# Another 20-product scheme for the first matmul of a convolution + GELU network, on one Trainium2 core

## The chip, the cores and the metric

The kernel runs on one core of one Trainium2 chip. The metric is the device time of one launch in microseconds (us). Engines are named as the profile names them: PE is TensorE (matmuls), PEld its weight loads, DVE is VectorE, ACT is ScalarE, POOL is GpSimd, SP is the queue that issues most DMA transfers. All data is float32. A matmul writes into a bank of the accumulation memory; there are eight banks, and here they go in four pairs. DVE and ACT read and write banks and ordinary memory; POOL and DMA only ordinary memory.

## The reference

```python
def _attn_ref(x, weight):            # x (8, 4096, 192), weight (8, 7)
    ...                              # softmax of each head's 7 taps
    out = np.einsum('hk,bskhg->bshg', w, x_unf)   # causal convolution of 7 taps
    return out.reshape(B, S, D)

def _moe_ref(x, w_in, w_out):        # x (32768, 192), w_in (192, 2048), w_out (2048, 192)
    h = x @ w_in
    g = h * (1.0 / (1.0 + np.exp(-1.702 * h)))
    return g @ w_out
```

A short convolution along the sequence, then a product with a 192 x 2048 matrix, a GELU, and a product with a 2048 x 192 matrix.

## The kernel before, in words

**Steps.** The 32768 tokens are done in 32 steps ("bigs") of 1024 tokens. A step has two parts: the first product with its GELUs (line 597), and the second product (line 1021). Step 0 and the start of step 1 are written out separately (`first_step`) and also prepare the weights. From step 2 on all steps have the same instructions.

**The first product by a fast scheme.** It is a product of block matrices of the convolved input (`conv_t`, blocks 0 to 5) by blocks of `w_in`, done twice in a step: half v = 0 and half v = 1 of the hidden columns. In place of 24 block products a half does 20, after a scheme of the Strassen kind: `TERMS[t]` says which combination of weights (`w_in_s`) is multiplied with which combination of input blocks. The combinations of input blocks are formed once a step on POOL (`SUMS_C`, called "vsum" in the lists; blocks 6 and up), those of weights once a launch on DVE (`SUMS_W`). One of the six input blocks (`OPEN`) is needed one half earlier than the others by the next step; one (`UNUSED`) enters sums only. Each block is also copied to the other 64 partitions by DMA (`cross`, on SP), because one product is two matmuls, each on 64 rows of the array:

```python
for h in range(2):
    src = pair[halves[h], ::-1, :] if h else pair[halves[h], :, :]
    nc.tensor.matmul(slot[h], w_in_s[halves[h], a, v * P : (v + 1) * P], src, start=first, stop=True, ...)
```

The two matmuls of a product write the two banks of a pair, h = 0 and h = 1. In float32 each matmul takes two passes, so one product is four PE and four PEld records.

**The list FIRST.** What is done with the products stands in `FIRST`, in the order in which it is issued, with names a0, a1, ... for pairs of banks and k0, k1, ... for places in memory (`room`, given by `ROOM_OF`). `("prod", t, a)` adds product t into a pair. `("copy", dst, src, sign)` copies a pair of banks on ACT, two instructions at line 632; copied to a place k it is kept for a later sum, copied to another pair a it becomes the seed on which further products accumulate. `("sum", dst, a, op, b)` adds or subtracts on DVE, two instructions at line 638. `("gelu", ...)` is on ACT: two instructions (line 614) from a pair of banks, one instruction of 1024 columns (line 619) from a place k. When a pair of banks has been used for the last time it goes to a list of free pairs, first in first out. Each engine works through its own queue in the order of issue and waits on semaphores. The first number of an item says how far ahead it is issued: an item with 1 or 2 is issued inside the half before, so that half v + 1 begins while half v ends; at the turn of a step the items with 1 wait until after the second part.

**Other work between the items.** `FILL[v]` says before which item of FIRST what else is issued: "tap" (one ACT multiplication of the convolution for a later step, line 488), "add" (a POOL addition of such taps, line 506), "vsum" (a POOL sum of blocks), "turn" (a DVE transpose of input, line 443; it also brings the rest of the taps and the end of the convolution, with the `cross` of the OPEN block, if they are still to be issued), "g" (a sum of GELU results for the second product, 128 x 1024 on DVE; one of the five is an accumulating DMA issued by POOL), "cross" (the DMA copies).

**The second part** goes through `PLAN`, a list of the same manner: 78 "go" (three main matmuls and a side matmul each), DVE sums and joins, ACT copies and taps. It takes three pairs of banks, in the order of the list of free pairs: the first is used by the first main and side matmuls at once. At its end up to all but the last of the remaining taps are issued.

Of the kernel before, what the change touches and what calls it, by code (L numbers as in the profile page):

```python
# [15 lines left out]
def kernel(  # L16
# [80 lines left out]
    g = consts.tile([P, NG, 2, 2, NG, T], F32)  # L97
# [29 lines left out]
    def kept(i):  # L127
# [11 lines left out]
    NV = 11  # L139
    NB = NBLK + NV  # L140
    UNUSED = 4
    OPEN = 2
    OPEN_SUM = None
# [5 lines left out]
        (6, 0, "-", 4), (7, 6, "-", 5), (8, 1, "+", 7), (9, 3, "+", 8), (10, 0, "-", 7), (11, 9, "-", 6),  # L149
        (12, 2, "-", 10), (13, 2, "-", 4), (14, 13, "+", 11), (15, 0, "+", 14), (16, 14, "-", 1),  # L150
# [15 lines left out]
    def side(big, other, b):  # L166
# [13 lines left out]
        (13, 9), (6, 14), (9, 0), (14, 5), (11, 6), (7, 2), (1, 3), (15, 3), (0, 0), (4, 16), (16, 8), (10, 2),  # L180
        (17, 15), (18, 7), (2, 11), (8, 12), (3, 1), (12, 1), (5, 10), (19, 13),
# [319 lines left out]
    tree, adds = [], []  # L501
# [138 lines left out]
    def plain(u, m, n, v, slot, ks=range(NC), first=0):  # L640

        for k in ks:
# [15 lines left out]
    ]  # L658
    ROOM_OF = ((0, 4, 1, 1, 4, 4, 4), (3, 0, 2, 2, 0, 2, 1))
# [3 lines left out]
            0: (("tap",),), 1: (("add", 4),), 2: (("add", 4), ("tap",)), 6: (("add", 4),), 11: (("turn", 0),),  # L663
            25: (("turn", 1),), 30: (("turn", 2),),
        },
        {
            0: (("g", 0), ("vsum",)), 1: (("vsum",), ("vsum",)), 2: (("vsum",),), 6: (("vsum",),), 7: (("vsum",),),
            14: (("g", 1), ("vsum",)), 15: (("g", 2),), 19: (("g", 3), ("vsum",), ("vsum",)), 21: (("g", 4),),
            22: (("vsum",),), 26: (("vsum",),), 38: (("cross",),),
# [4 lines left out]
            0: (("add", 12),), 1: (("work", 0.8),), 10: (("work", 0.8), ("tap",)), 15: (("work", 0.8),),  # L674
            19: (("tap",),), 21: (("work", 0.8),), 25: (("tap",),), 27: (("work", 0.8),), 30: (("tap",), ("tap",)),
            31: (("work", 0.8),), 38: (("tap",),), 40: (("tap",),), 42: (("work", 0.8),),
        },
        {
            5: (("g", 0),), 6: (("g", 1),), 13: (("turn", 0),), 19: (("g", 2), ("g", 3)), 21: (("g", 4),),
            26: (("turn", 1),), 27: (("turn", 2),),  # L680
# [259 lines left out]
    def store(big, n, o=None, queues=(nc.sync,) * 3):  # L940
# [16 lines left out]
        ("sum", 14, 14, "-", 18), ("side", 13, 16, "k0"), ("main", 1, 5, "p2", 1), ("vsum",), ("go", 2), ("tap",),  # L957
# [13 lines left out]
        ("sum", 6, 9, "-", 5), ("acc", 18, 14), ("tap",), ("go", 1), ("main", 20, 0, "p1", 0), ("tap",), ("go", 1),  # L971
# [8 lines left out]
        ("main", 8, 8, "p1", 0, 0, 2), ("tap",), ("tap",), ("tap",), ("tap",), ("tree",), ("go", 1),  # L980
# [10 lines left out]
        ("turn", 1, 1, 0, "k8"), ("store", 1, 0),  # L991
    ]
# [360 lines left out]
```

## Time and profile before

| what | value |
|---|---|
| median of 3 runs | 2288.6 us (2288.19 to 2289.3) |
| the profiled execution | 2288.38 us; its span in the trace 2286.6 us; granted PE clock 0.996 |
| PE busy | 2265.5 us, 99% |
| PEld busy | 1352.9 us, 59% |
| DVE busy | 1897.3 us, 83% |
| ACT busy | 1778.2 us, 78% |
| POOL busy | 1062.4 us, 46% |

In rows of groups and of the timeline, a line gives the kernel's line, engine, operation, written and read tiles, shape and count; then busy time and mean duration, or start and duration; and the idle time before with what ended it ("<-ACT room L632": the wait ended when line 632 on ACT had written room). "x2" is two merged instructions.

### The profile page before, as it was taken

The page shows a single profiled execution, that of the slowest core. Times are in us where ns is not written, and L with a number is a line of the kernel's source. Part 1 is how long each engine was busy: PE and PEld are TensorE (multiplying, and loading weights), DVE is VectorE, ACT ScalarE, POOL GpSimd, SP SyncE. Part 2 cuts the span into 40 slices and gives each one's busy share as a digit, 9 for nine tenths or more (in the row PEclk, how much of TensorE's full clock was granted, in tenths as well). Part 3 has the DMA queues.
Part 4 walks back from the last instruction along what each step waited for, and adds up shares of the span by engine and source line. Part 5 has one row for each costly group of instructions (what it writes and reads, how often), then busy time and mean ns, then how long its engine had stood idle before and what let it go on. Part 6 is the DMA issues. An engine that isn't in the chain of part 4 may idle for free.

```text
span 2286.6 us, 62092 instructions
## 1 busy us (share of the span) xinstructions
PE 2265.5 (99%) x24966; PEld 1352.9 (59%) x24966; DVE 1897.3 (83%) x2842; ACT 1778.2 (78%) x3481; POOL 1062.4 (46%) x1101
## 2 busy tenths in 40 slices
PE   9899999999999999999999999999999999999999
PEld 5356656666556566566665566665666655666655
DVE  8798888877888878888878888788888788887788
ACT  8568878788877788787788777887777887778855
POOL 1445544555435555445554355554455544555410
PEclk9899999999999999999999999999999999999999
DMA  9966577666586665776665866666766658664543
GB/s 200 156 146 137 113 141 148 131 126 122 115 161 135 128 127 114 139 147 133 128 123 112 161 138 126 126 116 135 151 133 127 123 112 159 139 128 99 104 94 71
DMA packets 281072, 298.84 MB, mean 131 GB/s; under 512 B 120144, under 2 KB 212304, under 8 KB 280784
## 3 DMA queue, kind: packets, MB, share of 16 engines
q0 software_dynamic: 58080, 151.48, 36.8%
q1 hardware_dynamic: 221056, 143.00, 28.0%
q8 instruction: 197, 3.23, 0.6%
q14 instruction: 91, 0.75, 0.1%
q10 hardware_dynamic: 1648, 0.39, 0.1%
HBM read 53.15 MB, written 25.17 MB: 34 GB/s over the span
## 4 chain that ended last, share of the span: by engine, by line
PE 95%; DVE 3%; ACT 1%; DMA 1%; issue 0%; SPq 0%; DVEq 0%; ACTq 0%
PE slot L597 48%; PE slot L1021 45%; PE slot L839 1%; DMA xin<-in_x_dram 0%; DVE g L363 0%; PE slot L844 0%; DVE xt L443 0%; ACT g L614 0%; DMA w_in_s<-in_moe_w_out_dram 0%; DVE w_in_s L363 0%; DVE conv_t L474 0%; DMA conv_t<-conv_t 0%; ACT w_form L488 0%; DVE slot L638 0%; ACT room L632 0%
## 5 line engine op out<-in xcount | busy, mean ns | idle before, releaser
L597 PE MATMUL slot<-conv_t,w_in_s 64*128 64x512 f32 x5152 | 1165.1, 599 | 3.9 <-ACT room L632 2.3
L597 PEld LDWEIGHTS slot<-conv_t,w_in_s 64*128 64x128 f32 x5152 | 700.2, 186 | 455.9 <-issue 227.3
L1021 PE MATMUL slot<-g,w_form 128*32 128x256 f32 x9672 | 896.0, 380 | 3.4 <-DVE room L361 3.4
L1021 PEld LDWEIGHTS slot<-g,w_form 128*32 128x32 f32 x9672 | 485.1, 110 | 164.4 <-DVE room L361 3.9
L506 POOL TENSOR_TENSOR conv_t<-conv_t,g 128x512 f32<-128x512 f32 x354 | 451.5, 1282 | 170.6 <-ACT g L488 149.7
L638 DVE TENSOR_TENSOR slot<-slot,room 128x512 f32<-128x512 f32 x496 | 320.6, 692 | 204.7 <-ACT g L614 118.5
L614 ACT ACTIVATE g<-slot 128x512 f32<-128x512 f32 x776 | 422.8, 613 | 75.1 <-PE slot L597 75.0
L1021 PE MATMUL slot<-g,w_out_s 128*32 128x256 f32 x5952 | 467.3, 379 | 0.0
L363 DVE TENSOR_TENSOR g<-g 128x1024 f32<-128x1024 f32 x372 | 453.0, 1243 | 3.2 <-DMA g<-osbs 1.0
L1046 ACT COPY room<-slot 32x256 f32<-32x256 f32 x651 | 238.3, 366 | 248.5 <-PE slot L1021 235.1
L488 ACT ACTIVATE g<-xt,cw 128x512 f32<-128x512 f32 x534 | 357.0, 716 | 4.0 <-DVE g L363 0.3
L632 ACT COPY room<-slot 128x512 f32<-128x512 f32 x620 | 337.7, 615 | 22.8 <-PE slot L597 21.8
L1021 PEld LDWEIGHTS slot<-g,w_out_s 128*32 128x32 f32 x5952 | 241.5, 110 | 188.8 <-ACT g L619 23.5
L997 POOL DMA_DIRECT2D g<-g x124 | 117.1, 950 | 354.5 <-PE slot L1021 184.9
L363 POOL TENSOR_TENSOR conv_t<-conv_t 128x256 f32<-128x256 f32 x210 | 181.5, 872 | 140.0 <-PE slot L597 73.9
L1021 PE MATMUL slot<-osbs,w_form 128*32 128x256 f32 x2232 | 225.3, 379 | 0.2 <-ACT room L1050 0.2
L511 POOL DMA_DIRECT2D g<-g x120 | 104.7, 889 | 251.7 <-ACT g L488 78.8
L638 DVE TENSOR_TENSOR slot<-room,slot 128x512 f32<-128x512 f32 x248 | 159.6, 689 | 40.1 <-PE slot L597 38.9
L632 ACT COPY slot<-slot 128x512 f32<-128x512 f32 x248 | 135.9, 572 | 55.0 <-PE slot L597 54.0
L619 ACT ACTIVATE g<-room 128x1024 f32<-128x1024 f32 x124 | 132.9, 1072 | 56.4 <-DVE room L638 56.4
L638 DVE TENSOR_TENSOR room<-slot,room 128x512 f32<-128x512 f32 x248 | 158.2, 678 | 22.3 <-ACT room L632 22.0
L1021 PEld LDWEIGHTS slot<-osbs,w_form 128*32 128x32 f32 x2232 | 117.3, 110 | 43.0 <-ACT room L1050 0.6
(171 smaller groups left out, 1691.6 us busy)
## 6 DMA issues: line engine op xcount, KB each, us to landing
g<-g POOLq DMA_DIRECT2D x124, 512.0 KB, 5.8
xin<-in_x_dram SPq DMA_DIRECT2D x240, 180.0 KB, 4.2
conv_t<-conv_t SPq DMA_DIRECT2D x186, 192.0 KB, 5.4
g<-g POOLq DMA_DIRECT2D x120, 256.0 KB, 5.0
out_dram<-osbs SPq DMA_DIRECT2D x186, 128.0 KB, 3.5
conv_t<-conv_t SPq DMA_DIRECT2D x124, 128.0 KB, 3.3
g<-room POOLq DMA_DIRECT2D x31, 512.0 KB, 5.5
conv_t<-g POOLq DMA_DIRECT2D x60, 256.0 KB, 5.7
```

Of the source, the lines that this page charges most:

```text
L363: eng.tensor_sub(v(dst), v(a), v(b))
L488: act.mul(home, conv_src(big, c, k), cw[:, c, k : k + 1])
L506: nc.gpsimd.tensor_add(dst, dst, home)
L511: nc.gpsimd.dma_start(out=out, in_=src, accum_op=ALU.add)
L597: nc.tensor.matmul(slot[h], w_in_s[halves[h], a, v * P : (v + 1) * P], src, start=first, stop=True, skip_group_check=True,)
L614: act.activation(dst[:, :, h, :], src[h].rearrange("p (o t) -> p o t", o=2), AF.Gelu_apprx_sigmoid, scale=float(sign),)
L619: act.activation(dst.rearrange("p o h t -> p h o t"), src.rearrange("p h (o t) -> p h o t", o=2), AF.Gelu_apprx_sigmoid, scale=float(sign),)
L632: act.copy(bank(dst, h), bank(src, h))
L638: op(*(bank(t, h) for t in (dst, a, b)))
L997: nc.gpsimd.dma_start(out=spot(dst), in_=spot(a), accum_op=ALU.add)
L1021: nc.tensor.matmul(dst, w, t, start=first, stop=last, skip_group_check=True)
L1046: act.copy(to, d)
```

## The change

Lists only; no function changes. `TERMS`, `SUMS_C`, `SUMS_W` hold other combinations: 10 sums of blocks a step in place of 11, plus one (`OPEN_SUM`) that is done on POOL just before the cross copy of the OPEN block (on DVE in step 1); 24 sums of weights a launch in place of 23. `FIRST` has 20 products as before, 9 sums in place of 8 and 6 copies in place of 7; one copy goes from bank to bank in place of two. Four of the eight GELUs read a place k in place of two. `FILL` and `PLAN` issue the same kinds of work at other places: two more taps stand at the end of the second part, "turn" comes at items 2, 16 and 40 of half 0 in place of 11, 25 and 30. The order of main and side matmuls in `PLAN` is the same.

```diff
-    NV = 11
+    NV = 10
-    UNUSED = 4
-    OPEN = 2
-    OPEN_SUM = None
+    UNUSED = 3
+    OPEN = 3
+    OPEN_SUM = (3, 3, '+', 1)
...
     TERMS = [
-        (13, 9), (6, 14), (9, 0), (14, 5), (11, 6), (7, 2), (1, 3), (15, 3), (0, 0), (4, 16), (16, 8), (10, 2),
-        (17, 15), (18, 7), (2, 11), (8, 12), (3, 1), (12, 1), (5, 10), (19, 13),
+        (7, 3), (9, 0), (16, 1), (3, 7), (12, 4), (17, 2), (10, 6), (18, 11), (2, 5), (0, 10), (1, 13), (14, 4),
+        (11, 8), (4, 15), (6, 1), (8, 5), (13, 9), (19, 0), (5, 12), (15, 14),
     ]
...
     FIRST = [
-        (0, "gelu", 2, 1, "a0", 1), (0, "sum", "a3", "a4", "-", "k1"), (0, "prod", 18, "a2"),
-        (0, "copy", "k0", "a2", 1), (0, "prod", 14, "a1"), (0, "sum", "a5", "k1", "-", "a1"), (0, "prod", 17, "a3"),
-        (0, "prod", 3, "a4"), (0, "prod", 16, "a5"), (0, "gelu", 3, 1, "a3", 1), (0, "prod", 1, "a1"),
-        (0, "gelu", 1, 0, "a5", 1), (0, "sum", "a6", "k0", "-", "a4"), (0, "prod", 15, "a6"), (0, "prod", 7, "a4"),
-        (0, "copy", "a7", "a6", 1), (0, "prod", 5, "a7"), (0, "gelu", 1, 1, "a4", 1), (0, "prod", 19, "a6"),
-        (0, "gelu", 0, 1, "a7", 1), (0, "sum", "a8", "a1", "-", "k2"), (0, "prod", 12, "a8"),
-        (0, "copy", "k3", "a6", 1), (0, "sum", "k4", "a8", "+", "k3"), (2, "prod", 11, "a0"), (0, "prod", 9, "a1"),
-        (1, "copy", "a2", "a0", 1), (0, "gelu", 2, 0, "k4", 1), (1, "prod", 0, "a2"),
-        (0, "sum", "a1", "a1", "+", "k3"), (1, "copy", "k2", "a2", 1), (1, "prod", 4, "a0"), (0, "prod", 8, "a8"),
-        (1, "prod", 10, "a2"), (1, "copy", "k6", "a0", 1), (0, "gelu", 0, 0, "a8", 1),
-        (0, "sum", "k5", "a1", "-", "k0"), (1, "sum", "a4", "a2", "-", "k6"), (1, "prod", 6, "a9"),
-        (1, "prod", 2, "a0"), (1, "prod", 13, "a4"), (0, "gelu", 3, 0, "k5", -1), (1, "copy", "k1", "a9", 1),
+        (0, "prod", 16, "a0"), (0, "sum", "a1", "a2", "-", "k0"), (0, "prod", 14, "a3"), (0, "copy", "k1", "a0", 1),
+        (0, "prod", 9, "a2"), (0, "sum", "a4", "a2", "-", "k1"), (0, "prod", 3, "a1"), (0, "copy", "k2", "a1", 1),
+        (0, "prod", 15, "a3"), (0, "prod", 7, "a4"), (0, "prod", 1, "a1"), (0, "sum", "k3", "a4", "+", "k4"),
+        (0, "sum", "k5", "a1", "-", "k1"), (0, "prod", 18, "a2"), (0, "gelu", 1, 1, "a3", 1), (0, "prod", 10, "a4"),
+        (0, "gelu", 3, 1, "k3", 1), (0, "prod", 17, "a1"), (0, "copy", "a5", "a4", -1), (0, "copy", "k6", "a2", 1),
+        (0, "prod", 19, "a4"), (0, "prod", 11, "a1"), (0, "prod", 8, "a5"), (0, "sum", "a6", "k6", "-", "a4"),
+        (0, "prod", 5, "a4"), (0, "gelu", 0, 1, "a1", 1), (2, "prod", 0, "a3"), (0, "gelu", 1, 0, "a5", 1),
+        (0, "sum", "a7", "a4", "+", "k2"), (0, "gelu", 2, 1, "k5", 1), (0, "prod", 4, "a6"), (0, "prod", 13, "a4"),
+        (0, "sum", "k7", "a7", "-", "k6"), (1, "copy", "k8", "a3", 1), (0, "sum", "k9", "a4", "-", "k0"),
+        (0, "gelu", 0, 0, "a6", 1), (0, "gelu", 2, 0, "k7", 1), (1, "prod", 6, "a8"),
+        (1, "sum", "k0", "a8", "-", "k8"), (1, "prod", 2, "a3"), (1, "copy", "k4", "a3", 1),
+        (0, "gelu", 3, 0, "k9", 1), (1, "prod", 12, "a2"),
     ]
...
     FILL = [
         {
-            0: (("tap",),), 1: (("add", 4),), 2: (("add", 4), ("tap",)), 6: (("add", 4),), 11: (("turn", 0),),
-            25: (("turn", 1),), 30: (("turn", 2),),
+            0: (("tap",), ("tap",), ("tap",), ("tap",), ("add", 4)), 2: (("add", 4), ("turn", 0)), 12: (("add", 4),),
+            16: (("turn", 1),), 40: (("turn", 2),),
         },
         {
-            0: (("g", 0), ("vsum",)), 1: (("vsum",), ("vsum",)), 2: (("vsum",),), 6: (("vsum",),), 7: (("vsum",),),
-            14: (("g", 1), ("vsum",)), 15: (("g", 2),), 19: (("g", 3), ("vsum",), ("vsum",)), 21: (("g", 4),),
-            22: (("vsum",),), 26: (("vsum",),), 38: (("cross",),),
+            0: (("vsum",),), 4: (("g", 0),), 7: (("vsum",), ("vsum",), ("vsum",), ("vsum",)), 10: (("vsum",),),
+            13: (("g", 1),), 15: (("g", 2),), 17: (("g", 3),), 18: (("vsum",),), 20: (("vsum",),), 22: (("vsum",),),
+            26: (("g", 4),), 32: (("vsum",),), 40: (("cross",),), 42: (("cross",),),
         },
     ]
```

From step 2 on a half of the changed kernel has its products in the order P6, P2, P12, P16, P14, P9, P3, P15, P7, P1, P18, P10, P17, P19, P11, P8, P5, P0, P4, P13, where P0 belongs to the half after. The kernel before has, in the first half of a step, P0, P4, P10, P6, P2, P13, P18, P14, P17, P3, P16, P1, P15, P7, P5, P19, P12, P11, P9, P0, and so on; there P11 belongs to the half after, and P0, P4, P10 are again that half's first products, with P8 between P4 and P10.

More of the change, by code (lines that the diff above doesn't have):

```diff
@@ L148 @@
     SUMS_C = [
-        (6, 0, "-", 4), (7, 6, "-", 5), (8, 1, "+", 7), (9, 3, "+", 8), (10, 0, "-", 7), (11, 9, "-", 6),
-        (12, 2, "-", 10), (13, 2, "-", 4), (14, 13, "+", 11), (15, 0, "+", 14), (16, 14, "-", 1),
+        (6, 2, "-", 3), (7, 0, "+", 6), (8, 7, "-", 4), (9, 3, "+", 8), (10, 5, "+", 8), (11, 1, "+", 10),
+        (12, 11, "-", 0), (13, 11, "-", 9), (14, 2, "+", 13), (15, 1, "+", 6),
     ]
@@ L645 @@
     FIRST = [
[12 rows of a table removed]
[12 rows of a table added]
     ]
-    ROOM_OF = ((0, 4, 1, 1, 4, 4, 4), (3, 0, 2, 2, 0, 2, 1))
+    ROOM_OF = ((4, 0, 3, 2, 1, 1, 0, 1, 1, 2), (0, 1, 4, 2, 3, 3, 2, 3, 3, 2))
     FILL = [
         {
-            0: (("tap",),), 1: (("add", 4),), 2: (("add", 4), ("tap",)), 6: (("add", 4),), 11: (("turn", 0),),
-            25: (("turn", 1),), 30: (("turn", 2),),
-        },
-        {
-            0: (("g", 0), ("vsum",)), 1: (("vsum",), ("vsum",)), 2: (("vsum",),), 6: (("vsum",),), 7: (("vsum",),),
-            14: (("g", 1), ("vsum",)), 15: (("g", 2),), 19: (("g", 3), ("vsum",), ("vsum",)), 21: (("g", 4),),
-            22: (("vsum",),), 26: (("vsum",),), 38: (("cross",),),
+            0: (("tap",), ("tap",), ("tap",), ("tap",), ("add", 4)), 2: (("add", 4), ("turn", 0)), 12: (("add", 4),),
+            16: (("turn", 1),), 40: (("turn", 2),),
+        },
+        {
+            0: (("vsum",),), 4: (("g", 0),), 7: (("vsum",), ("vsum",), ("vsum",), ("vsum",)), 10: (("vsum",),),
+            13: (("g", 1),), 15: (("g", 2),), 17: (("g", 3),), 18: (("vsum",),), 20: (("vsum",),), 22: (("vsum",),),
+            26: (("g", 4),), 32: (("vsum",),), 40: (("cross",),), 42: (("cross",),),
         },
@@ L673 @@
         {
-            0: (("add", 12),), 1: (("work", 0.8),), 10: (("work", 0.8), ("tap",)), 15: (("work", 0.8),),
-            19: (("tap",),), 21: (("work", 0.8),), 25: (("tap",),), 27: (("work", 0.8),), 30: (("tap",), ("tap",)),
-            31: (("work", 0.8),), 38: (("tap",),), 40: (("tap",),), 42: (("work", 0.8),),
-        },
-        {
-            5: (("g", 0),), 6: (("g", 1),), 13: (("turn", 0),), 19: (("g", 2), ("g", 3)), 21: (("g", 4),),
-            26: (("turn", 1),), 27: (("turn", 2),),
+            0: (("add", 12),), 1: (("work", 0.8),), 8: (("work", 0.8),), 9: (("tap",),), 16: (("work", 0.8),),
+            19: (("tap",),), 21: (("tap",), ("work", 0.8)), 27: (("work", 0.8),), 28: (("work", 0.8),),
+            30: (("tap",),), 31: (("tap",),), 34: (("tap",),), 42: (("work", 0.8), ("tap",)),
+        },
+        {
+            5: (("g", 0),), 8: (("g", 1),), 13: (("turn", 0),), 15: (("g", 2),), 19: (("turn", 1),), 20: (("g", 3),),
+            24: (("turn", 2),), 29: (("g", 4),),
         },
@@ L956 @@
     PLAN = [
-        ("sum", 14, 14, "-", 18), ("side", 13, 16, "k0"), ("main", 1, 5, "p2", 1), ("vsum",), ("go", 2), ("tap",),
[13 rows of a table removed]
-        ("sum", 6, 9, "-", 5), ("acc", 18, 14), ("tap",), ("go", 1), ("main", 20, 0, "p1", 0), ("tap",), ("go", 1),
[8 rows of a table removed]
-        ("main", 8, 8, "p1", 0, 0, 2), ("tap",), ("tap",), ("tap",), ("tap",), ("tree",), ("go", 1),
[8 rows of a table removed]
[13 rows of a table added]
+        ("side", 8, 8, "k1", 2, 4), ("acc", 7, 10), ("sum", 13, 18, "+", 4), ("acc", 18, 14), ("main", 2, 5, "p4", 0),
+        ("sum", 6, 9, "-", 5), ("vsum",), ("go", 1), ("tap",), ("go", 2), ("tap",), ("tap",), ("tree",), ("go", 1),
[5 rows of a table added]
+        ("main", 21, 7, "p2", 0), ("go", 2), ("side", 7, 20, "k1"), ("vsum",), ("tap",), ("tree",), ("go", 2),
[6 rows of a table added]
+        ("join", "k7", "k4", "-", "p4"), ("tap",), ("tap",), ("tap",), ("tap",), ("tap",), ("go", 1),
[4 rows of a table added]
         ("join", "k2", "p2", "-", "k4"), ("turn", 0, 0, 1, "k1"), ("store", 0, 1), ("go", 1), ("turn", 0, 1, 1, "k2"),
```

63 rows, old and new, of tables (PLAN, SUMS_W) are left out of this document.

## The prediction

> **What bounds the kernel now.** I read the page first, then the chain that ended last, then the timeline of the weight loads in one step.
>
> ```profile
> span 2286.6 us, 62092 instructions
> PE 2265.5 (99%) x24966; PEld 1352.9 (59%) x24966; DVE 1897.3 (83%) x2842; ACT 1778.2 (78%) x3481; POOL 1062.4 (46%) x1101
> ```
>
> The profiled execution took 2288.38 us, 1.8 us more than its span and 0.2 us less than the median of the three runs (2288.6), so I take the sum against 2288.4. The three runs lie within 1.1 us; 0.2% (4.6 us) is about the least difference that a measurement can tell from no change.
>
> By these rows PE is full, and the change leaves its 24966 matmul records alone. But a matmul's record is long because matmuls overlap, so I look for lost time in the loads.
>
> ```profile
> 955.81 35.99 PE slot L597 x158
> 1025.61 36.00 PE slot L597 x158
> ```
>
> ```profile
> 1025.54 0.30 PEld L597 LDWEIGHTS slot<-conv_t,w_in_s 64*128 64x128 f32 x4 [0.41 <-issue]
> 1026.07 0.19 PEld L597 LDWEIGHTS slot<-conv_t,w_in_s 64*128 64x128 f32 x2 [0.23 <-issue]
> 1027.48 0.29 PEld L597 LDWEIGHTS slot<-conv_t,w_in_s 64*128 64x128 f32 x2 [0.78 <-ACT room L632]
> 1027.96 0.29 PEld L597 LDWEIGHTS slot<-conv_t,w_in_s 64*128 64x128 f32 x3 [0.19 <-ACT room L632]
> 1028.44 0.24 PEld L597 LDWEIGHTS slot<-conv_t,w_in_s 64*128 64x128 f32 x2 [0.18 <-issue]
> 1028.87 0.24 PEld L597 LDWEIGHTS slot<-conv_t,w_in_s 64*128 64x128 f32 x2 [0.18 <-issue]
> ...
> 1038.03 0.29 PEld L597 LDWEIGHTS slot<-conv_t,w_in_s 64*128 64x128 f32 x2 [0.26 <-ACT slot L632]
> 1038.52 0.29 PEld L597 LDWEIGHTS slot<-conv_t,w_in_s 64*128 64x128 f32 x3 [0.20 <-ACT slot L632]
> 1061.53 0.12 PEld L1021 LDWEIGHTS slot<-g,w_out_s 128*32 128x32 f32 x3 [0.76 <-ACT g L619]
> ```
>
> The first fence is of the chain (start, us, what), the second of the loads' timeline. A step is 69.80 us, its first part 36.0. In the loads, undisturbed pairs come every 0.429 us (1028.44, 1028.87): two row halves together, two pairs a product, so 0.858 us a product. A step's first part has 40 products, 34.33 us; from 1025.54 to 1061.53 it takes 35.99. So 1.66 us a step is lost inside "busy" PE, 30 x 1.66 = 50 us over steps 2 to 31. That is all that this change can win there, and only as banks come back sooner.
>
> The Trainium skill, page "Trainium Kernel Development and Optimization", section Performance Expectations, says that matmul busy time is a bad metric for the distance to the roofline, because matmuls are pipelined; the trace agrees, with 1.66 us a step lost under 99%.
>
> Where it is lost: 0.10 as the array refills (1026.07 stands 0.53 after the first load, not 0.43). Then P10, the third product, waits for the copy of P0's banks with one product between: its loads would begin at 1025.54 + 0.10 + 1.72 = 1027.36, but begin at 1027.48 for the first row half and 1027.96 for the second, 0.12 and 0.60 late, and each late start adds a refill of 0.05 to 0.10. From there on the second half runs 0.4 behind the first, and so its later evictions are awaited with more patience. P5 at 1038.03, again one product behind a copy, loses only some 0.15. There are four such places a step (P10; P5 in both halves; P0 behind P11), and the last chain, GELU then sum, costs 0.1 twice. The sum of these is 0.10 + 0.65 + 3 x 0.13 + 2 x 0.12, about 1.4; the rest is lost in the last product (0.17) and at the hand-over to the second part (0.10).
>
> **How soon a bank comes back.** Durations:
>
> ```profile
> L597 PE MATMUL slot<-conv_t,w_in_s 64*128 64x512 f32 x5152 | 1165.1, 599 | 3.9 <-ACT room L632 2.3 <-ACT g L614 1.2 <-DVE w_in_s L346 0.3
> L614 ACT ACTIVATE g<-slot 128x512 f32<-128x512 f32 x776 | 422.8, 613 | 75.1 <-PE slot L597 75.0
> L632 ACT COPY room<-slot 128x512 f32<-128x512 f32 x620 | 337.7, 615 | 22.8 <-PE slot L597 21.8
> L638 DVE TENSOR_TENSOR slot<-slot,room 128x512 f32<-128x512 f32 x496 | 320.6, 692 | 204.7 <-ACT g L614 118.5 <-PE slot L597 84.2 <-ACT room L632 1.1
> L632 ACT COPY slot<-slot 128x512 f32<-128x512 f32 x248 | 135.9, 572 | 55.0 <-PE slot L597 54.0
> L619 ACT ACTIVATE g<-room 128x1024 f32<-128x1024 f32 x124 | 132.9, 1072 | 56.4 <-DVE room L638 56.4
> L363 DVE TENSOR_TENSOR g<-g 128x1024 f32<-128x1024 f32 x372 | 453.0, 1243 | 3.2 <-DMA g<-osbs 1.0
> L506 POOL TENSOR_TENSOR conv_t<-conv_t,g 128x512 f32<-128x512 f32 x354 | 451.5, 1282 | 170.6 <-ACT g L488 149.7
> L363 POOL TENSOR_TENSOR conv_t<-conv_t 128x256 f32<-128x256 f32 x210 | 181.5, 872 | 140.0 <-PE slot L597 73.9 <-DVE osbs L361 63.7 <-issue 2.3
> ```
>
> ```profile
> 1012.14 1.95 ACT L488 ACTIVATE g<-xt,cw 128x512 f32<-128x512 f32 x3
> 1025.70 0.36 ACT L1046 COPY room<-slot 32x256 f32<-32x256 f32 x1 [0.28 <-PE slot L1021]
> 1026.09 0.72 ACT L488 ACTIVATE g<-xt,cw 128x512 f32<-128x512 f32 x1
> 1026.84 2.05 ACT L632 COPY room<-slot 128x512 f32<-128x512 f32 x4
> ```
>
> ```profile
> 1026.89 0.44 DVE L937 STREAM_TRANSPOSE osbs<-room 96x256 f32<-96x256 f32 x1
> 1028.71 1.30 DVE L638 TENSOR_TENSOR slot<-slot,room 128x512 f32<-128x512 f32 x2 [1.37 <-PE slot L597]
> 1047.66 1.39 DVE L363 TENSOR_TENSOR g<-g 128x1024 f32<-128x1024 f32 x1
> 1061.39 1.28 DVE L638 TENSOR_TENSOR room<-slot,room 128x512 f32<-128x512 f32 x2
> ```
>
> A product's banks are complete 0.43 + 0.60 = 1.02 us after its first load. A copy or GELU frees the first bank 0.60 later and the second 0.51 after that (2.05 us for four); a DVE sum 0.69 and 0.61 (1.30 for two). Reaction is about 0.05 on ACT and 0.1 on DVE. With one product between, the next user is due at 1.72: a copy frees its banks at 1.67 and 2.18, so the second is late. With two between, due at 2.57, a copy has 0.4 to spare and a sum 0.15 (2.42). So distance two costs nothing if the queue ahead is empty.
>
> **The change, walked in that way.** Times count from the step's first load; product n is due at 0.858 (n - 1) + 0.10.
> - Removed: P10's wait, the three other waits behind a copy at distance one, and the last chain.
> - Start of a step. Three taps now stand on ACT before P2's copy to k4, where one stood. They start at 0.55 (1025.70 + 0.36) and take 1.95: to 2.50. The copy then frees the banks at 3.13 and 3.64; P14, fifth product, is due at 3.53. Second half late 0.12, with refill 0.22. A fourth tap and the transpose behind it, to 4.3 and 5.1, are clear of P9's sum (5.5). DVE is busy with the output until 1.79 as before (1026.89 + 0.44); sum k0 then ends at 3.0, sum a1 at 4.25, P9 is due at 4.4: free.
> - P7 is due 6.97 behind a sum done at 6.83; P1, P10: free likewise. Sum k5 queues behind k3 (8.1 to 9.4) and ends at 10.6; P17's second bank is due at 10.6: 0.10.
> - P19 is the only product at distance one, behind P10's copy a5, once in each half. P10 is complete at 10.56, the banks free at 11.19 and 11.70, P19 due at 11.26 and, with the lag collected by then, 11.58: 0.21. In the second half the lag is larger: 0.08.
> - GELU a5, sum a7, sum k7, P6 of the next half: 14.9, 16.35, 17.55 against 17.8 due. Free with 0.2 to spare. P9 of the second half stands behind the transpose and a1 (22.03 against 22.1): 0.08.
> - Second half, DVE: k5 ends at 27.8, g sums 1 and 3 take 2.3 (to 30.1), sum a6 frees a4 at 30.7 and 31.3, P5 is due at 31.2 and 31.7. Free with 0.4 to spare. g 4, a7, k7 end at 34.85, the second part starts at 35.2 in the bank pair that k7 frees; its fifth "go" needs k9's (36.2 against 36.9). Free.
>
> Loss: 0.10 + 0.22 + 0.10 + 0.21 + 0.08 + 0.08 = 0.79, and 0.10 at the hand-over as before. Second part at 34.33 + 0.89 = 35.22, not 35.99: 0.77 us less a step. One price is unknown: the copy a5 is now a multiplication by -1 between banks. No row shows it; the nearest are the copy between banks (572), the GELU from a bank (613) and the tap (716). I take the GELU's, 0.04 more for each half's P19, so 0.70 a step (0.77 at one end; at the tap's end, 0.14 for each bank, 0.35 to 0.4).
>
> POOL, SP. Twelve adds of 1.28 after the last tap (4.3) end near 20.2 and the new sum at 21.1; the OPEN block's transfer must be there for P0 at 32, some 11 us later:
>
> ```profile
> conv_t<-conv_t SPq DMA_DIRECT2D x186, 192.0 KB, 5.4
> ```
>
> It is hidden; without that cover P0 would wait up to 6. On SP behind this transfer stand only input loads for a later step. One block sum fewer on POOL and two fewer transfers a step: off the path.
>
> Second part: DVE has 30.7 of 33.8 us busy there, in the same sums and joins; two taps leave it. DVE enters it 0.97 after its start, before 1.13 (1061.39 + 1.28 - 1061.53). I take it as unchanged.
>
> ```profile
> 1043.50:1061.50 18.00, 18.00 (x83) 12.50 (x79) 16.11 (x24) 15.01 (x28) 12.86 (x15) 1.00 0.74 161
> 1061.50:1095.30 33.80, 33.80 (x625) 20.17 (x624) 30.74 (x45) 26.11 (x55) 9.45 (x12) 1.00 0.79 151
> ```
>
> ```profile
> 107.95 2.06 ACT L632 COPY room<-slot 128x512 f32<-128x512 f32 x4
> 108.59 0.29 PEld L597 LDWEIGHTS slot<-conv_t,w_in_s 64*128 64x128 f32 x2 [3.13 <-ACT room L632]
> ```
>
> (The windows' columns are PE, PEld, DVE, ACT, POOL.) In step 1 PE waits 3.13 us for a copy that ACT starts at 107.95, because the third product needs it. After, the fifth does: some 1.7 (two products) less. Against it the weights' one more sum (0.4) and more sums on a DVE that is as full as above. I take -1, from -2.5 to +2.
>
> Sum: 2288.4 - 30 x 0.70 - 1 = 2266.4, say 2266.
>
> **Rivals.**
> - *DVE late in the second half* (slower). That half has 16.1 of 18 us busy on DVE, and one sum more (1.3) fills it. If g 1 and g 3 take longer than 2.3 together, sum a6 is late, and P5 waits. It begins to cost from 0.4 late; 1.2 late eats the whole gain. The row at 1047.66 (1.39 where others take 1.22) shows that beside POOL's sums it can be 0.17. Were each of the two g's held for a whole POOL sum (872), 1.74 late, P5 would lose 1.3: +0.6 a step, 2288.4 + 18 - 1 = 2305. Against it: of four g's before, one was slower, by 0.17. The Trainium skill, page "SBUF — State Buffer", section Who interferes with whom, has the rule for it: a VectorE instruction with two SBUF inputs and a GpSimd one that reads SBUF exclude each other, the second fully blocked. By that rule the g's, not the sums from banks, would be held. Chance 0.13.
> - *Nothing to win*: the second part gives back what the first wins, since DVE there is 91% busy and a sum that comes late stops a main matmul; or the plan's new places cost 0.7 a step. Before shows no such loss (78 "go" in 33.8). 2288. Chance 0.12.
> - *More than that*: P14, P17 and the two terms of 0.08 cost nothing, because the evictions run a little earlier than I put them. 0.4 more a step: 2266 - 12 = 2254. Chance 0.08.
> - That the change doesn't do what it says is not one: the order of each engine's instructions is as in the lists.
>
> **How the numbers follow.** Forecast (2257 to 2280: gain 0.25 to 1.0 a step) 0.67, and the three rivals 0.13, 0.12, 0.08. Likeliest: 2266. The low end is the third rival's 2254, less 1 for the first stage; the high end takes in the second rival with a first stage worse by 2: 2290. Left out are most of the first rival and the lowest tail, under 0.2. Faster by over 0.2% (below 2284): forecast and third rival, 0.75. Within: 0.11 of the second rival. Slower: 0.14.
>
> **What would show it.** In the loads of the first part after: no idle above 0.3 us at a third product; a wait at the fifth (P14, 0.1 to 0.2) and at P19 behind ACT line 632 or its negative form; the second part starting 35.2 after the first load; a step of 69.1. Wrong if the step's spacing stays at 69.8 or grows, if P5 of the second half waits for DVE, or if the loads of the second part show gaps.

## The result, and the profile after

The changed kernel takes 2275.8 us (median; 2275.3 to 2276.4), the kernel before, run beside it, 2289.0: ratio 0.9941, 95% interval 0.9924 to 0.9959, so 13.2 us or 0.6% faster. The forecast was 2266 (range 2253 to 2290): the direction is right, the gain a little over half of what the sum gave.

The profiled execution took 2275.51 us, 12.9 less than before's. The page after, span and first row of part 1:

```profile
span 2273.7 us, 62148 instructions
PE 2252.5 (99%) x24966; PEld 1564.5 (69%) x24966; DVE 1985.3 (87%) x2967; ACT 1709.2 (75%) x3233; POOL 1069.9 (47%) x1101
```

As many matmuls as before, PE still at 99%. The loads' share rose from 59% to 69% while the time fell; the reason is in the second part, below. One step in the chain that ended last (start, us, what), and the same step in the loads' timeline:

```profile
1089.22 35.41 PE slot L597 x157
1124.63 33.94 PE slot L1021 x624
```

```profile
1089.15 0.30 PEld L597 LDWEIGHTS slot<-conv_t,w_in_s 64*128 64x128 f32 x4 [0.41 <-issue]
1089.69 0.19 PEld L597 LDWEIGHTS slot<-conv_t,w_in_s 64*128 64x128 f32 x2 [0.23 <-ACT room L632]
...
1092.42 6.90 PEld L597 LDWEIGHTS slot<-conv_t,w_in_s 64*128 64x128 f32 x33 [0.39 <-ACT room L632]
...
1100.47 0.29 PEld L597 LDWEIGHTS slot<-conv_t,w_in_s 64*128 64x128 f32 x2 [0.40 <-POOL conv_t L506]
1100.94 0.29 PEld L597 LDWEIGHTS slot<-conv_t,w_in_s 64*128 64x128 f32 x3 [0.18 <-ACT slot L634]
...
1117.77 0.29 PEld L597 LDWEIGHTS slot<-conv_t,w_in_s 64*128 64x128 f32 x2 [0.20 <-ACT slot L634]
1118.27 0.29 PEld L597 LDWEIGHTS slot<-conv_t,w_in_s 64*128 64x128 f32 x3 [0.21 <-ACT slot L634]
...
1123.51 0.29 PEld L597 LDWEIGHTS slot<-conv_t,w_in_s 64*128 64x128 f32 x2 [0.29 <-DVE slot L638]
1124.56 0.15 PEld L1021 LDWEIGHTS slot<-g,w_out_s 128*32 128x32 f32 x6 [0.76 <-DVE room L638]
1124.71 0.14 PEld L1021 LDWEIGHTS slot<-g,w_form 128*32 128x32 f32 x2
1124.80 0.12 PEld L1021 LDWEIGHTS slot<-g,w_out_s 128*32 128x32 f32 x3
1124.96 0.11 PEld L1021 LDWEIGHTS slot<-g,w_form 128*32 128x32 f32 x1
```

The wait at the third product is gone. There is one at the fifth (1092.42: P14 behind the copy to k4), one at P19 in each half (1100.47, 1117.77, behind the copy a5, line 634; the first of its rows is put down to GpSimd's adds, but the wait goes when that copy is left out, in e9 below), and one at the last product (1123.51). The first part takes 35.41, where it took 35.99. The second part takes 33.94, where it took 33.81: its side matmuls (w_form in the rows above) now start 0.15 behind the mains and stay there. A load takes 110 ns as before, but those of the sides no longer lie on top of those of the mains, so that PEld counts as busy for 28.7 us of a second part and no longer for 20.2; that is its higher share.

A step is 69.36 in place of 69.80. From step 2's first load to that of the last step the kernel won 10.0 us (2014.3 for 2024.3); 2.5 came before step 2's first load, 0.4 after the last step's.

### The profile page after: what moved, and what is told of

It reads as the page before. It is cut to its first block, busy times and chain, and to the rows that moved or that the text cites. A ratio compares the mean times of both kernels' runs of the same rounds, so it can differ in the third digit from the quotient of the medians.

```text
span 2273.7 us, 62148 instructions
## 1 busy us (share of the span) xinstructions
PE 2252.5 (99%) x24966; PEld 1564.5 (69%) x24966; DVE 1985.3 (87%) x2967; ACT 1709.2 (75%) x3233; POOL 1069.9 (47%) x1101
## 4 chain that ended last, share of the span: by engine, by line
PE 92%; DVE 4%; DMA 2%; ACT 1%; issue 1%; POOL 0%; DVEq 0%; POOLq 0%; ACTq 0%; SPq 0%
PE slot L597 47%; PE slot L1021 45%; DVE g L363 1%; DMA conv_t<-conv_t 1%; DMA xin<-in_x_dram 0%; PE slot L839 0%; DMA g<-osbs 0%; DMA conv_t<-w_form 0%; DVE room L363 0%; DVE w_in_s L363 0%; DMA w_in_s<-in_moe_w_out_dram 0%; DVE slot L638 0%; DVE osbs L937 0%; DVE conv_t L474 0%; PE slot L1113 0%
## 5 line engine op out<-in xcount | busy, mean ns | idle before, releaser
L597 PE MATMUL slot<-conv_t,w_in_s 64*128 64x512 f32 x5152 | 1148.5, 595 | 2.2 <-DVE slot L638 1.4
L597 PEld LDWEIGHTS slot<-conv_t,w_in_s 64*128 64x128 f32 x5152 | 669.5, 186 | 468.3 <-issue 304.9
L1021 PEld LDWEIGHTS slot<-g,w_form 128*32 128x32 f32 x9672 | 576.3, 110 | 129.3 <-DVE room L363 1.7
L638 DVE TENSOR_TENSOR room<-slot,room 128x512 f32<-128x512 f32 x620 | 383.7, 680 | 67.0 <-PE slot L597 66.7
L619 ACT ACTIVATE g<-room 128x1024 f32<-128x1024 f32 x248 | 265.6, 1071 | 79.6 <-DVE room L638 50.2
L614 ACT ACTIVATE g<-slot 128x512 f32<-128x512 f32 x528 | 283.1, 609 | 51.5 <-PE slot L597 32.2
L638 DVE TENSOR_TENSOR slot<-slot,room 128x512 f32<-128x512 f32 x372 | 239.8, 689 | 53.9 <-PE slot L597 51.2
L1021 PEld LDWEIGHTS slot<-osbs,w_form 128*32 128x32 f32 x2232 | 132.4, 110 | 23.8
L638 DVE TENSOR_TENSOR slot<-room,slot 128x512 f32<-128x512 f32 x124 | 79.8, 688 | 43.0 <-PE slot L597 42.0
L1021 PE MATMUL slot<-room,w_form 128*32 128x256 f32 x1488 | 112.9, 379 | 0.4 <-DVE room L363 0.4
```

Of the source, the lines that this page charges most:

```text
L614: act.activation(dst[:, :, h, :], src[h].rearrange("p (o t) -> p o t", o=2), AF.Gelu_apprx_sigmoid, scale=float(sign),)
L619: act.activation(dst.rearrange("p o h t -> p h o t"), src.rearrange("p h (o t) -> p h o t", o=2), AF.Gelu_apprx_sigmoid, scale=float(sign),)
L638: op(*(bank(t, h) for t in (dst, a, b)))
L1021: nc.tensor.matmul(dst, w, t, start=first, stop=last, skip_group_check=True)
```

## Experiments

For the comparisons below I took, for each of a first part's 160 matmul records, its start less its place in an undisturbed row (0.429 a pair), as the median over 28 steps. "A" is the first row half and "B" the second (each has a bank of its own), in us, after the product named. The numbers in brackets count the products of a first part, 21 and up being the second half's:

```
                                 P14(5th)  13th       P19(14th)  22nd       35th       last, B   first part
changed kernel                   .10/.43   .10/.43    .30/.69    .33/.69    .47/.82    .99       35.42
e1  taps moved                   .10/.24   .51/.93    .61/1.01   .66/1.02   .80/1.16   1.33      35.76
e5  taps moved, k4's own room    .10/.11   .10/.37    .30/.69    .33/.69    .47/.82    .99       35.42
e9  no copy a5                   .10/.42   .10/.42    .10/.42    .17/.53    .17/.53    .83       35.25
e10 e5 without copy a5           .10/.11   .10/.37    .10/.37    .17/.53    .17/.53    .83       35.26
                                 3rd       8th        17th       22nd       36th       last, B
before                           .39/.76   .46/.89    .67/1.05   .89/1.17   1.01/1.31  1.57      35.99
e12 before, no copy to k2        .10/.11   .24/.66    .44/.82    .67/.95    .79/1.07   1.35      35.77
```

Theory: B falls 0.3 to 0.4 behind A at the first late bank (the lag) and stays there; a later late bank costs B only what exceeds that, and both halves a refill (what the passes just behind a late start lose in addition, 0.05 to 0.2 in this table). So lateness is paid for once. Rival: the places add up.

**e1: the taps away from P14.**

```
-        while len(ready) > 2 and big > 1:
+        while len(ready) > 5 and big > 1:
-  0: (tap, tap, tap, tap, add 4), 2: (add 4, turn 0), 12: (add 4), ...
+  0: (tap, add 4), 2: (add 4), 4: (tap, tap), 8: (tap, turn 0), 12: (add 4), ...
```

> From the changed kernel: of the taps that stand on ACT ahead of P2's copy to k4 at the start of a step, none is left there; one stands behind that copy, two behind P16's copy, one behind P3's, and the first transpose of the half follows them. So P14, the fifth product, finds its banks. Theory (a late bank is paid for once: the second row half falls some 0.5 us behind the first and stays there, and a place that comes later costs only what it adds to that and the refill): P14's delay (the second row half goes from 0.11 to 0.43) is gone, but P19 then takes the second row half to 0.6 to 0.7 in any case. First part 35.3 to 35.42, step 69.25 to 69.36, time 2272 to 2276. Rival (the places add up): 0.22 to 0.32 less a step, step 69.05 to 69.14, time 2266 to 2269. A third: the taps in their new places make a copy late, and the step grows.

2297.4 us, ratio 1.0035 (1.0021 to 1.0048); typical first part 35.76, and seven steps are 0.8 to 2.2 longer still, for a reason that e5 shows. In one step (first load 1028.22), ACT's copy to k4, then VectorE:

```profile
1030.55 1.18 ACT L632 COPY room<-slot 128x512 f32<-128x512 f32 x2 [1.70 <-DVE room L638]
1036.32 0.78 DVE L443 STREAM_TRANSPOSE xt<-xin 128x576 f32<-128x576 f32 x1 [1.27 <-issue]
1037.02 2.44 DVE L638 TENSOR_TENSOR room<-slot,room 128x512 f32<-128x512 f32 x4
```

The third case came true, by way of the transpose: in its new place it stands ahead of sum k3 (line 638), and P10 and P17 wait for that (A 0.51, B 0.93 by the 13th product). But the row of P19 is telling: met with 0.43 of lag it costs A 0.10 and B 0.08, where in the changed kernel, met with 0.32, it costs 0.20 and 0.26. And the copy to k4 (1030.55) still starts 2.33 after the step's first load, with no tap ahead of it: its room is that of k8, which sum k0 on VectorE still reads.

**e2: two places more.** e1 with P14 and P16 exchanged (`prod 14, prod 16` for `prod 16 ... prod 14`).

> The same, and P14 and P16 change places in both halves, so that P14 stands at distance one behind P2's copy to k4: two more places of the kind of which the change took two away. Theory (paid once): each place takes the second row half to some 0.6 behind, and P19 finds it there; only refills are added, 0.05 to 0.15 a place: first part 35.4 to 35.6, step 69.35 to 69.55, time 2275 to 2281. Rival (the places add up, 0.5 as P10's in the kernel before): two places, 1.0 a step more than the run without the swap, step above 70.0, time above 2295.

2348.3 us, ratio 1.0250 (1.0237 to 1.0264); first part 37.15, 1.4 above e1. Neither number holds. P14, now fourth, comes so much too early that its first bank is late as well: A 0.56 and B 0.69 more than in e1 there, A 0.44 and B 0.34 in the second half; the other 0.4 is lost at P10 and P17, whose wait has grown. A lag of B does nothing for a late A. The theory needs that limit: only what falls on B alone, up to the lag, is paid once.

**e5: P14 alone, cleanly.** e1 with the transpose behind sum k5 and k4 in another room than k8's (k2 and k3 change places for it):

```
-  ROOM_OF = ((4, 0, 3, 2, 1, 1, 0, 1, 1, 2), ...
+  ROOM_OF = ((4, 0, 2, 3, 3, 1, 0, 1, 1, 2), ...
-  8: (tap, turn 0), 12: (add 4),
+  8: (tap), 12: (add 4), 13: (turn 0),
```

> From the changed kernel: the taps moved as in the first run, the first transpose put behind sum k5 (so that k3 and k5 aren't held), and k4 put in another room than k8, so that P2's copy to k4 no longer waits for sum k0. The copy can then start at P2's end, 2.0 after the first load in place of 2.6, and P14 finds its banks. Theory (a late bank is paid for once): P14's 0.32 is gone at the fifth product, but P19 takes the second row half from 0.11 to 0.6 to 0.7 in any case, and all that follows is as before: first part 35.3 to 35.42, step 69.25 to 69.36. Rival (the places add up): first part 35.1, step 69.04.

P14's 0.32 is gone (0.10/0.11), P17, hidden until then, takes B to 0.37, P19 to 0.69, and from there every figure is that of the changed kernel:

```profile
1089.94 35.41 PE slot L597 x157
1125.35 33.94 PE slot L1021 x624
```

So the theory, to 0.01 us. The time is 2284.1 nevertheless, because eleven steps are 0.8 to 1.7 longer. In one of them (first load 740.36), VectorE and GpSimd:

```profile
741.17 2.16 DVE L361 TENSOR_TENSOR room<-room 96x256 f32<-96x256 f32 x1
743.37 0.44 DVE L937 STREAM_TRANSPOSE osbs<-room 96x256 f32<-96x256 f32 x1
743.74 1.25 DVE L638 TENSOR_TENSOR room<-slot,room 128x512 f32<-128x512 f32 x2
```

```profile
741.46 7.05 POOL L506 TENSOR_TENSOR conv_t<-conv_t,g 128x512 f32<-128x512 f32 x5
```

The output's last sum, two SBUF inputs, takes 2.16 where the changed kernel has 0.38, while GpSimd runs its adds; k0, a1 and P3 are late behind it. In this step the adds start 1.1 after the first load, while that sum runs. In e5's steps of the usual length they start 1.28 or more after it, when the sum is done (1.19); in all eleven long ones it is 0.84 to 1.13. In the changed kernel they start 4.4 after the first load, behind the last tap. The taps kept GpSimd away; I had not seen that.

**e9 and e10: P19 without its copy**, on the changed kernel and on e5's: `(0, "copy", "a5", "a4", -1)` struck out.

> From the changed kernel: the copy of a4 to a5 with sign -1 is left out in both halves, and P8 starts a5 afresh (the output lacks that seed, so its time is that of the wait and not of a whole computation; ACT has two copies less each half). P19 then has no bank to wait for, P14 still has. Theory (paid once): the 0.43 that P14 left to the second row half stays to the end, P19's 0.26 and 0.14 go: 0.43 + the 0.17 at the last product, first part 35.0 to 35.05, step 68.9 to 69.0. Rival (the wait at P19 is another's, GpSimd's adds or a sum): first part above 35.25.

> The same on the kernel with the taps moved and k4 in a room of its own, which by itself left the first part at 35.41: now neither P14 nor P19 finds a late bank (the same seed is left out). Theory (paid once): now taking away P14's late bank pays, since nothing later collects it again: first part 34.6 to 34.75 (34.33 + 0.10 + 0.17 at the last product + 0.1 at the hand-over), 0.3 to 0.4 below the run without the taps moved, where with the copy in place the same move gave 0.00. Rival (the taps' move is worth nothing by itself): first part 35.0.

2271.8 us (0.9924; 0.9910 to 0.9938) and 2279.0 (0.9957; 0.9944 to 0.9969, with e5's long steps). Typical steps of each:

```profile
1087.90 35.25 PE slot L597 x158
1123.15 33.94 PE slot L1021 x624
```

```profile
1016.35 35.25 PE slot L597 x158
```

Both numbers miss: I had 35.0 to 35.05 and 34.6 to 34.75. With P19 out of the way, P6 of the second half (B 0.53) and the last product (0.13, then its 0.17) collect what P19 had covered, and in e10 P17 does so before them. The copy's two places cost 0.40 where they stand and are worth 0.17 at the end; P14's costs 0.32 and is worth nothing, with the copy or without. That is the theory once more, and I had not followed it far enough when I wrote the numbers.

**e12: the dearest place of the kernel before.** `(1, "copy", "k2", "a2", 1)` struck out of the kernel before, so that P10, the third product, finds its banks.

> From the kernel before: the copy of P0's banks to k2 is left out (the sum that reads k2 gets an old value, so its time is that of the wait and not of a whole computation), so that P10, the third product, the dearest of the places that the change removed, has no bank to wait for; all other places stay. Rival (the places add up, as the prediction's walk of the kernel before did: 0.65 of its 1.66 at this place): first part 35.3 to 35.45, step 69.1 to 69.25, nearly all that the change won. Theory (paid once: a late bank costs the last row half nothing as long as a later place is late by as much; what stays of each place is the refill): P14, P5 and the others behind it find the second row half in time and collect the same lateness: first part 35.75 to 35.95, step 69.55 to 69.75.

2286.6 us, 0.9983 (0.9974 to 0.9992; what comes before step 2 takes 4.2 us longer than in the kernel before). Typical step:

```profile
1097.53 35.77 PE slot L597 x159
1133.30 33.81 PE slot L1021 x624
```

35.77, 0.22 less, as the theory said. The place cost A 0.28 and B 0.65; P14's place behind it, 0.13 in the kernel before, now costs B 0.55. So the dearest place alone is worth 0.22 of the 0.58 that the change won in the first part. With all of the change's places together, A's delay at the end fell from 1.14 to 0.47, and B's from 1.57 to 0.99.

**e4: the second part's 0.13.**

```
-        bx, bs, by = (free.pop(0) for _ in range(3))
+        bs, by, bx = (free.pop(0) for _ in range(3))
```

> From the changed kernel: the second part takes its three bank pairs in another order: its first main and side use the pair that the GELU of a6 frees, the next the pair of k7, the last that of k9. Theory: the first load of the second part no longer waits for k7's second bank, and the side matmuls start close behind the mains: second part 33.8, hand-over 0.1 to 0.2 earlier, P13's 0.17 stays: step 69.0 to 69.2, time 2265 to 2271. Rival (the second part's 0.13 comes from its own list): second part 33.94, step 69.2 to 69.36, time 2271 to 2276.

2274.0 us, 0.9927 (0.9914 to 0.9939).

```profile
1087.23 35.42 PE slot L597 x157
1122.65 33.81 PE slot L1021 x624
```

```profile
1121.53 0.29 PEld L597 LDWEIGHTS slot<-conv_t,w_in_s 64*128 64x128 f32 x2 [0.30 <-DVE slot L638]
1122.58 0.12 PEld L1021 LDWEIGHTS slot<-g,w_out_s 128*32 128x32 f32 x3 [0.76 <-ACT g L614]
1122.60 0.11 PEld L1021 LDWEIGHTS slot<-g,w_form 128*32 128x32 f32 x1
```

The side stands 0.02 behind the main and the second part is back at 33.81: the 0.13 was that pair, whose second bank sum k7 gives back last. The hand-over did not move: its 0.76 of idle is the same whatever releases the bank, and what comes before it is the last product's own lateness. The time is 1.8 below the changed kernel's (the two were not run side by side). Of the 0.13 x 29 = 3.8 us that a step's sum promised, 2.3 are there from step 2's first load to the last step's: five second parts are 0.1 to 0.6 longer, and in the three longest a VectorE sum waits 0.5 to 0.8 for the accumulating DMA of g 2. The last step takes 1.3 longer; its hand-over has 1.55 of idle.

**e3 and e11: g 4 behind k9.** `26: (g 4)` becomes `35: (g 4)`; e11 adds e4's line and turns one sum of the second part into an accumulating DMA:

```
-        ("sum", 11, 7, "+", 11)
+        ("acc", 11, 7)
```

> From the changed kernel: in the second half the last block sum of g (g 4) stands on VectorE behind k9 and no longer ahead of a7. Theory: P13's wait for a7's second bank (0.17 at the 40th product), the wait of the second part's first load for k7 and the 0.13 by which the side matmuls run behind all come from g 4 ahead of a7 and k7. First part 35.1 to 35.25, second 33.8, step 68.9 to 69.05, time 2261 to 2267. Rival A (the second part's 0.13 comes from its own new list): first part the same, second 33.94, step 69.1, time 2268. Rival B (VectorE, 90% busy in the second part, has no room for 1.2 us more there): second part over 34.2, time as the changed kernel's or above.

> From the changed kernel: the bank pairs of the second part in the other order (second part 33.81 in the run with that alone), g 4 behind k9 (first part 35.32 in the run with that alone, and 0.28 more in the second part, since a block sum of g came late there), and one in-place block sum of the second part (spot 11 += spot 7) done by an accumulating DMA in place of VectorE, which takes the 1.2 us back that g 4 brings into the second part. Theory: first part 35.3, second 33.81, step 69.1 to 69.15, time 2266 to 2270. Rival (the DMA queues, 0.75 busy there, make the accumulated block late, or the sums before it are late as before): second part 34.0 to 34.5, time 2274 to 2285.

e3: 2281.9 us (0.9962; 0.9950 to 0.9974), first part 35.32 and second 34.22: its rival B. The last product's second pass is 0.07 late and no longer 0.17 (a7 starts 0.6 earlier there), but in the second part the loads wait 0.69 for a VectorE sum:

```profile
1126.78 0.12 PEld L1021 LDWEIGHTS slot<-g,w_out_s 128*32 128x32 f32 x3 [0.76 <-DVE room L638]
1146.19 1.45 PEld L1021 LDWEIGHTS slot<-g,w_form 128*32 128x32 f32 x32 [0.69 <-DVE room L363]
1161.00 0.30 PEld L597 LDWEIGHTS slot<-conv_t,w_in_s 64*128 64x128 f32 x4 [0.41 <-issue]
```

e11: 2270.0 us (2268.3 to 2270.5), 0.9917 (0.9903 to 0.9930), faster than the kernel before. It was not run side by side with the changed kernel, and the intervals of the two ratios overlap a little; but the slowest of its four runs is 4.8 us below the fastest of the changed kernel's, and its typical step is 35.32 + 33.81 for 35.41 + 33.94. The page:

```profile
span 2266.6 us, 62066 instructions
PE 2246.7 (99%) x24966; PEld 1323.6 (58%) x24966; DVE 1942.9 (86%) x2936; ACT 1704.1 (75%) x3233; POOL 1071.5 (47%) x1132
```

**e8 and e6: the slower rival made real.** e8 puts g 4 ahead of sum a6; e6 is e4 with g 2 moved from place 15 to 23, behind three of GpSimd's block sums.

> From the changed kernel: g 4 stands on VectorE ahead of sum a6 in the second half, and no longer behind it: the prediction's slower rival made real, a6 1.2 to 1.7 late where 0.4 is to spare. Theory (price as in the prediction: from 0.4 late it costs): P5 of the second half waits 0.7 to 1.2, less what the second row half already lags (0.4): 0.4 to 1.2 a step, and P13's wait goes: step 69.6 to 70.5, time 2283 to 2308. Rival (other slack absorbs it): step 69.2 to 69.4, time 2271 to 2276.

> The kernel with the bank pairs of the second part in another order, and in the second half g 2 (the accumulating DMA that GpSimd issues, which waits for g 1) put behind three of GpSimd's block sums, which then run some 1.5 us earlier, beside g 1 and g 3, and no longer beside g 4. Theory (the block sums on GpSimd hold g 4: 1.68 where 1.22 is usual, so a7 comes late and P13 waits): g 4 takes 1.22, P13's 0.17 falls below 0.05, first part 35.25, second 33.81, step 69.06; g 1 or g 3 are held instead, by up to 0.4 together, which sum a6 has to spare. Rival (P13 waits for a7 whatever g 4 takes, or a6 gets late and P5 waits): first part 35.41 or above, step 69.23 or above.

e8: 2349.7 us (1.0259; 1.0245 to 1.0273), first part 37.99. VectorE, then the loads, of one step (first load 1122.57):

```profile
1152.90 2.76 DVE L363 TENSOR_TENSOR osbs<-osbs,g 128x1024 f32<-128x1024 f32 x1
1155.59 1.28 DVE L638 TENSOR_TENSOR slot<-room,slot 128x512 f32<-128x512 f32 x2
```

```profile
1156.32 0.29 PEld L597 LDWEIGHTS slot<-conv_t,w_in_s 64*128 64x128 f32 x2 [2.63 <-DVE slot L638]
```

Sum a6 is 2.80 later in the step than in the changed kernel, and P5's first passes come A 2.39 and B 2.57 later: slack 0.4 and 0.2, where the prediction had 0.4. The size was wrong, since g 4 takes 2.76 beside GpSimd's DMA issue and two block sums. e6: 2286.2 us (0.9983; 0.9974 to 0.9992), first part 35.71: a6 is 0.52 later, P5 costs B 0.29 (its second parts are uneven too, 5 us in all); g 4 fell to 1.35, and the last product is 0.17 late as before. I had expected g 4's length to decide that; the run does not settle it, since a7 starts 0.2 later there all the same.

**e7: the first stage.** In step 1 the four sums of the second product go ahead of the new block sum (the loop with s4 and s3 stands before `need("done 1")`).

> From the changed kernel: in step 1 the four sums s3, s4 of the second product are issued to VectorE ahead of the new block sum and no longer behind it. Theory (the block sum waits there for the taps' adds by DMA and holds VectorE's queue, and the four sums behind it cost 1.7): step 1's first load comes 1.7 us earlier (105.6 for 107.3), all else as in the changed kernel, 2274. Rival (the first stage waits for something else, a DMA or the weights): first load at 107.3 still, 2275.8.

2275.7 us, as the changed kernel. The first load came at 105.95 for 107.34, but step 1's first part is 0.9 longer, waits for VectorE growing in it (one from 1.47 to 2.34), and step 2 starts only 0.5 earlier, step 3 0.3. The theory of the queue holds and has no worth.

## Why the prediction was right or wrong

*What bounds it* held: the change won in the first part, where banks come back sooner. Of its signs, the idle time at the third product went and the waits at P14 and P19 came; a step of 69.1 and a second part from 35.2 on did not (69.36 and 35.4).

*The first part.* The forecast was 35.22, with the price of the copy 35.30; it took 35.41. Term by term: fill 0.10 (0.10 measured), P14 0.22 (0.32), P17 0.10 (0), P19 0.25 (0.26), P9 of the second half 0.08 (0), P19 there 0.12 (0.14), hand-over 0.10 (0.09). The term that failed is the last product: the prediction counted 0.17 there in the kernel before and left it out of the sum for the changed one, where it is 0.17 too. With it the forecast was 35.39, or 35.47 with the copy's price. That the rest agrees is partly luck, P14 up by 0.10, two terms of 0.18 down.

*The copy a5* was priced as a GELU (613 ns a bank). It takes 581 on average, near the copy between banks (572), so the 0.04 that the price put on each P19 was not there; P19 came to 0.26 without it. Two banks, on ACT:

```profile
1117.14 1.08 ACT L634 ACTIVATE slot<-slot 128x512 f32<-128x512 f32 x2 [0.21 <-PE slot L597]
```

*P14.* The prediction had three taps in front of the copy to k4. So it is (first load 1089.15):

```profile
1089.81 1.95 ACT L488 ACTIVATE g<-xt,cw 128x512 f32<-128x512 f32 x3
1091.79 1.07 ACT L632 COPY room<-slot 128x512 f32<-128x512 f32 x2
```

But e1 and e5 show a second reason behind them, the room shared with k8: without the taps the copy starts 0.31 earlier, and only with a room of its own too is P14 on time. The walk looked at engines and banks and not at rooms.

*The sum itself* was walked as a list of losses that add up. e5, e9, e10 and e12 show that they don't: the row of places has a lag to fill, and the last places set the end. In the kernel before the list read 0.65 for P10, and P10 alone was worth 0.22. Walked in order with the lag carried along, as the prediction did for P19, the total comes out; a single term of it is no forecast for that term's removal.

*The second part*, which the prediction took as unchanged, lost 0.13 a step, 3.8 us. The prediction saw that the second part starts in the pair that k7 frees, but asked only when the first bank of it is free, and not the second, to which the first sides go; in e4, which starts in another pair, the 0.13 is gone.

*The first stage*: -1 forecast, -2.5 measured, at the end of the range given. Not as argued: the first load is 3.0 later, because the new block sum waits on VectorE for the taps' adds and four sums queue behind it (e7, where these go first, takes 1.4 of the 3.0 away); step 1 wins 5.6 back.

```profile
79.51 0.42 DVE L361 TENSOR_TENSOR conv_t<-conv_t 128x256 f32<-128x256 f32 x1 [10.65 <-DMA conv_t<-conv_t]
79.85 0.55 DVE L880 TENSOR_TENSOR conv_t<-w_out_s,w_form 128x384 f32<-128x384 f32 x1
```

*The steps that are not typical* were left out: step 2 is 1.5 longer than the others, and waits in a few more sum to 1.4. So 29 x 0.44 = 12.8 gave 10.0.

*Together*: from the forecast 2266.4 to the profiled 2275.5 it is 9.1 us. The first part has 3.5 of it (0.58 won and not 0.70), the second part 3.8, the untypical steps 2.8 and the last step 0.3, less the 1.5 that the first stage won beyond its forecast.

*The rivals.* "Nothing to win" has a part in it, the second part's 0.13. "VectorE late" did not come: sum a6 was on time. VectorE in the second half, then:

```profile
1116.90 1.40 DVE L361 TENSOR_TENSOR osbs<-g 128x1024 f32<-128x1024 f32 x1
1118.23 1.21 DVE L363 TENSOR_TENSOR osbs<-g 128x1024 f32<-128x1024 f32 x1
1119.37 1.28 DVE L638 TENSOR_TENSOR slot<-room,slot 128x512 f32<-128x512 f32 x2
1120.56 1.68 DVE L363 TENSOR_TENSOR osbs<-osbs,g 128x1024 f32<-128x1024 f32 x1
```

g 1 and g 3 took 2.5 together for 2.3, within the slack; g 4 was held (1.68), behind a6, where it comes ahead of a7 and k7: in e3, with g 4 moved away, the last product is 0.10 less late and the sides of the second part start 0.02 behind the mains.

Open is what makes the last product's second pass 0.17 late, in the kernel before and in all others but e3 and e11 (0.07), where a7 starts 0.6 sooner.

## What to carry to other kernels

Late buffers in a pipeline with two interleaved streams don't add up: walk them in order, carry the lag along, and judge an edit by what the next place will then collect. Where a later stage takes over buffers, ask for the last one that it needs and not the first, and let it start in those that were done longest. A busy share is no guide there: here the loads' share went from 59% to 69% as the time fell by 0.6%, and back to 58% as it fell further.

## What the runs showed of the hardware

A VectorE sum with both inputs in SBUF was stretched beside GpSimd from 0.38 to 2.16, and from 1.22 to 1.68 and 2.76; sums with one input in a bank stayed at 1.25 to 1.30 for two beside the same work. The Trainium skill, page "SBUF — State Buffer", section Who interferes with whom, has this as an exclusive lock of a port pair that VectorE shares with GpSimd; the trace agrees on which sums are held. What I had not expected is that the order of ACT's taps decides it, by the time at which GpSimd's adds may start.

At the switch from the 64-row loads to the 128-row ones the loads are idle for 0.76, in at least 30 of the 31 hand-overs of every kernel here, whoever is named as the releaser. Little of that is lost: the first matmul of the second part starts 0.52 after the last one of the first part, where 0.43 is the undisturbed distance, and this 0.09 is the hand-over's term in the sums above.
